# Attention masked by bias products in two batches instead of one, with another order of loads, copies and first products

## The chip, the cores and the metric

The kernel runs on one core of one Trainium2 chip. The metric is device time in microseconds (us). Three runs of the kernel before took 254.89, 254.92 and 255.02 us; the median is 254.92 us.

## The reference

The inputs are q, k and v of 8 batches, 8 heads, 576 positions and 64 values per head, and four matrices. All are float32. Cut to what matters:

```python
scores = matmul(q, k.T) / sqrt(64)
rel = pos[:, None] - pos[None, :]
mask_plain = (rel >= 0) & (rel < 32)                       # heads 0 to 3
mask_dil = (rel >= 0) & (rel < 128) & (rel % 4 == 0)       # heads 4 to 7
attn = softmax(where(mask, scores, -1e9))
x = matmul(attn, v)          # as 4608 tokens x 512
a, b = x @ w1, x @ w2        # 512 -> 1024
out = ((a * b) @ w3) @ w_out # 1024 -> 1024 -> 512
```

Each position sees 32 keys only: the last 32 (plain heads) or every fourth of the last 128 (dilated heads).

## The kernel before

**The layout.** The positions of each head are sorted by their remainder modulo 4, so that a dilated window becomes a run of 32 neighbours. Both kinds of heads are then cut into blocks of 96 queries that see 128 keys (96 and a halo of 32). A batch has 12 such blocks: six for the four plain heads (u = 0), six for the four dilated heads (u = 1). All multiplications are done in bfloat16.

**The work on a batch.** q, k and v are loaded by DMAs that the POOL queue issues and that convert to bfloat16. Batch 0's first halves of q and k come as float32 over the SP queue and are rounded by ScalarE. VectorE turns them (`turn`, L388 and L403: transposes of 32x32 blocks) so that the head's values lie across partitions. In batches 0 and 1, v is turned by VectorE too, then turned back by TensorE against an identity (`v_back`, L412), and copied to `vps` (`v_keep`: L422 on ScalarE, L424 on VectorE); these are the tasks VK. From batch 2 on (`DIRECT_V = 2`), v is loaded straight into place by many small DMAs.

TensorE makes scores for a group of blocks in four PSUM banks (`Group.scores`, L454). ScalarE takes the exponential (L465). A step is three blocks, four heads: TensorE multiplies the exponentials with v and a column of ones (`values`, L490), VectorE takes the reciprocal of the sums (L501) and scales (L513). In batches 0 and 1 (`TURNED = 2`) TensorE turns the step back (L530) and a copy puts it into the matrix of tokens XT (`Step.keep`: L538 on ScalarE, L540 on VectorE); these are the tasks K. From batch 2 on, a DMA issued by SP does it (L543).

**The masks.** There are two ways. Batches under `BIASED` are grouped by three blocks, and a matmul of the identity with a table of 0 and -30000 (`bias`) is put into the PSUM banks ahead of the scores (L437), so that the exponential of a masked score is 0. The other batches are grouped by five blocks across batch borders (`GRP = 5`), and VectorE multiplies the exponentials with a 0/1 mask, in two halves (L473). POOL makes that mask from the bias table (L367). The choice is made here:

```python
if biased:
    first = {(0, 0): 0, (0, 3): 1, (1, 0): 4, (1, 3): 4}[self.blocks[0][1:]]
    for g in range(4):
        nc.tensor.matmul(out=self.sp[:, g, 0 : self.n * QB], lhsT=ident,
            rhs=bias[:, first : first + self.n, :], start=True, stop=False)
...
if b < BIASED:
    for i in range(0, 12, 3):
        group(every[i : i + 3], True)
```

**The products.** w3 and w_out are multiplied once on the chip (w3 is turned by L647, copied by L654, multiplied by L659, and kept as `wf_sb` by L670 on ScalarE or L672 on VectorE; the tasks W3D). The tokens are worked off in 16 units of 288 columns, two for a batch. For each unit and each of eight pieces of 128 outputs, TensorE makes the up products a and b (L563, four matmuls of 288 columns each, over the four pieces of XT: two of plain heads, two of dilated heads), ScalarE copies a (L573), VectorE multiplies with b (L578). Down products of 128 tokens (L589, eight matmuls of 512 columns) follow when their gates and all of `wf_sb` are there; ScalarE copies them (L600) and SP stores them.

**What sets the order.** All instructions are recorded as tasks with a duration, dependences and a rank. A planner (`Plan.run`) takes, whenever an engine is free, the ready task of the lowest rank, gives out the eight PSUM banks, and puts filler matmuls (L701) where TensorE would be idle ahead of the first up product. The tasks are then written out in this order, and each engine takes its queue strictly in it. The constants at the head of the file steer it: `RANK` and `FIRST` give ranks by kind of task (`FIRST` for batch 0; E exponential, VK and K the copies, N reciprocal and scaling, T turns, VT v turned back, S scores, V values, X step turned back), `WARM` counts matmuls at the start (L684), `FIRST_LOADS` and `B0_LOADS` set the order of loads on POOL ("v10" is batch 1's v, first half; "w0" a piece of w1 and one of w2; "o0" half of w_out; "30" the first 128 rows of w3), `ON_DVE` names copies that VectorE makes, `HALVED` copies of which ScalarE makes one half and VectorE the other. `LEAD` sets which up products must go ahead of a batch's scores. `PARTED` is 0: an up product waits for all four pieces of XT.

```python
if k or parted == PARTED:
    return add(name, "PE", 490, need + wl, lambda: up(k, f, key), seq, slot=1,
               after=after), []
...
for b, i, t in paced:
    pair = int(16 * (b - LEAD) + 4 * i)
```

Of the kernel before, what the change touches and what calls it, by code (L numbers as in the profile page):

```python
# [19 lines left out]
S = 576  # L20
# [6 lines left out]
UNIT = 288  # L27
RING = 1152
BIG = 30000.0
BIASED = 1  # L30
LATE = False
TURNED = 2
DIRECT_V = 2
ORDER = (2, 3, 0, 1)
RES = (0, 2, 1, 3)
RANK = dict(E=0.5, VK=3, K=2, N=0.2, T=0.5, VT=0.05, S=0.1, V=0.05, X=0.1, W=0.5, C=5)
FIRST = {"E": 3, "VK": 1, "K": 0.2, "N": 2, "T": 0.2, "VT": 0.05, "S": 0.3, "V": 0.1, "X": 0.3}
WARM = 25
FILL = 110
FIRST_LOADS = ("30", "w0", "v10", "w1", "w2", "31", "k10", "q10", "o0", "o1", "32", "33", "34", "q11", "k11", "v11", "35", "36", "37")  # L40
SHIFT = {}
ON_DVE = ("K0.2", "VK0.1.1", "W3D1", "W3D4", "W3D5")
GRP = 5
WHOLE = ("qn", "kn")
B0_LOADS = ("v0", "q1", "k1", "v1")
HALVED = ("K0.0", "K0.1", "K0.3", "K1.1", "VK0.0.0", "VK0.1.0", "VK1.0.1", "VK1.1.0")
MASK_AT = 19.5
PARTED = 0
BUSY = 4500
LEAD = 1.1  # L50


class Task:
# [10 lines left out]
class Plan:  # L64
# [10 lines left out]
    def add(self, name, eng, dur, deps, fn, prio, slot=0, lat=150, after=()):  # L75
        t = Task(name, eng, dur, deps, fn, prio + SHIFT.get(name, 0), slot, lat, after)
        self.tasks.append(t)
        return t
# [108 lines left out]
def kernel(  # L187
# [51 lines left out]
    def bank(n, dtype=F32):  # L239
        at = ps[:, plan.now.place or 0, :]  # L240
        return (at if dtype == F32 else at.bitcast(dtype))[:, 0:n]
# [317 lines left out]
    def up(k, f, key, chunks=ORDER, first=True, last=True):  # L559
        if first:  # L560
            held[(key, k, f)] = bank(UNIT)
        for j, c in enumerate(chunks):
            nc.tensor.matmul(  # L563
                out=held[(key, k, f)],
                lhsT={"a": w1_sb, "b": w2_sb}[key][:, c, f * P : (f + 1) * P],
                rhs=unit_cols(k, c),
                start=(first and j == 0),
                stop=(last and j == len(chunks) - 1),
            )
# [74 lines left out]
    def w3_back(ft):  # L644
        x = bank(KFF * P, BF16).rearrange("p (g x) -> p g x", g=KFF)
        for g in range(KFF):
            nc.tensor.transpose(  # L647
                out=x[:, g, :], in_=w3n[ft][:, g * P : (g + 1) * P], identity=ident
            )
        held[("x3", ft)] = x  # L650

    def w3_keep(ft):
        w3T[ft] = wk_pool.tile([P, KFF, P], BF16, tag="w3T", bufs=3, name="w3T")
        nc.scalar.copy(out=w3T[ft], in_=held[("x3", ft)])  # L654
# [13 lines left out]
    def w3_done(ft, eng):  # L668
        if eng == "ACT":
            nc.scalar.copy(out=wf_sb[:, ft, :], in_=held[("wf", ft)])  # L670
        else:
            nc.vector.tensor_copy(out=wf_sb[:, ft, :], in_=held[("wf", ft)])  # L672
# [5 lines left out]
    def rank(kind, b):  # L678
        return (RANK if b else FIRST)[kind]

    def warm_up():
        o = bank(256)
        for i in range(WARM):
            nc.tensor.matmul(out=o, lhsT=warm[:, 0:P], rhs=warm, start=True, stop=True)  # L684
# [21 lines left out]
    c0 = add("const2", "DVE", 1400, [c1], constants, -98)  # L706
    add("warm", "PE", 700 + 213 * WARM, [c1], warm_up, 0)

# [11 lines left out]
    def loads_rows(nm, b, us=None):  # L720
        old = turned.get((nm, b - 2), [])
        for u in (0, 1) if us is None else us:
            L[(nm, b, u)] = None
        sl = slice(0, 2) if us is None else slice(us[0], us[-1] + 1)
        t = load(f"L{nm}{b}", 700, 3100 if us is None else 1600, old,
                 lambda: load_rows(nm, rows_of[nm], b, sl))
        for u in (0, 1) if us is None else us:
            L[(nm, b, u)] = t
# [25 lines left out]
    plan.dma = 1200 + 1350 * len(WHOLE)  # L754
    for x in B0_LOADS:
        loads_rows(x[0] + "n", 0, (int(x[1]),))
# [9 lines left out]
    lw12 = {}  # L766
    for x in FIRST_LOADS:
        c = int(x[1])
# [12 lines left out]
    for ft in sorted(lw3):  # L781
        x = add(f"W3T{ft}", "PE", 450, [lw3[ft], idt], lambda f=ft: w3_back(f), RANK["W"], slot=1,
                after=w3m[-3:-2])
        y = add("W3C", "ACT", 1012, [x], lambda f=ft: w3_keep(f), RANK["C"], lat=100, after=w3m[-3:-2])
        if ft + 7 in lw3:
# [4 lines left out]
        name = f"W3D{ft}"  # L790
        eng, dur = ("DVE", 688) if name in ON_DVE else ("ACT", 585)
        FUSED.append(add(name, eng, dur, [z], lambda f=ft, e=eng: w3_done(f, e), -1, lat=100))
# [28 lines left out]
    for b in range(B):  # L821
# [9 lines left out]
        for u in range(2):  # L831
# [3 lines left out]
            for half in range(2):  # L835
# [5 lines left out]
                name = f"VK{b}.{u}.{half}"  # L841
                eng, dur = ("DVE", 980) if name in ON_DVE else ("ACT", 880)
                ways = [(eng, dur, slice(0, 4))]
                if name in HALVED:
                    ways = [("ACT", 540, slice(0, 2)), ("DVE", 560, slice(2, 4))]
# [44 lines left out]
        every = [(b, u, m) for u in range(2) for m in range(6)]  # L890
        if b < BIASED:
            for i in range(0, 12, 3):
# [8 lines left out]
        while steps < 4 * B:  # L901
# [25 lines left out]
            if bb < TURNED:  # L927
                x = add("X" + n, "PE", 310, ns + [idt], st.back, bb - 99 + rank("X", bb), slot=1)
                name = f"K{n}"
                eng, dur = ("DVE", 460) if name in ON_DVE else ("ACT", 640)  # L930
                ways = [(eng, dur, slice(0, 6 * QB))]
                if name in HALVED:
                    ways = [("ACT", 400, slice(0, 3 * QB)), ("DVE", 270, slice(3 * QB, 6 * QB))]
# [14 lines left out]
    def ups(k, f):  # L948
# [8 lines left out]
        def product(key, after):  # L957
# [3 lines left out]
            seq += 1  # L961
            if k or parted == PARTED:
                return add(name, "PE", 490, need + wl, lambda: up(k, f, key), seq, slot=1,
# [47 lines left out]
    for b, i, t in paced:  # L1011
        pair = int(16 * (b - LEAD) + 4 * i)
        if pair > 0:
# [38 lines left out]
```

## Time and profile before

| what | value |
| --- | --- |
| median of three runs | 254.92 us |
| profiled execution: time | 255.02 us |
| profiled execution: span | 253.2 us |
| granted TensorE clock, mean | 0.998 |
| busy: PE / DVE / ACT / POOL | 245.8 / 167.9 / 124.3 / 67.8 us |
| matmuls | 2760 |
| up products L563 | 1024 matmuls, first at 20.27 us, last at 244.0 us |
| bias products L437 | 16 matmuls |
| mask passes L473 | 34, 21.2 us |
| exponentials L465 | 21, 34.2 us |
| DMA | 33.40 MB, 210 GB/s until about 50 us |

Spans and starts are counted from the first instruction of the profile. "Busy" is the time in which at least one instruction of an engine runs; matmuls overlap, so that the mean of one is longer than its share of the time. A row of the groups names the line, engine and operation, what it writes and reads, how often it stands, its busy time, the mean duration of one in ns, and the idle time of its engine just before it with what ended most of that.

### The profile page before, as it was taken

The page shows a single profiled execution, that of the slowest core. Times are in us where ns is not written, and L with a number is a line of the kernel's source. Part 1 is how long each engine was busy: PE and PEld are TensorE (multiplying, and loading weights), DVE is VectorE, ACT ScalarE, POOL GpSimd, SP SyncE. Part 2 cuts the span into 40 slices and gives each one's busy share as a digit, 9 for nine tenths or more (in the row PEclk, how much of TensorE's full clock was granted, in tenths as well). Part 3 has the DMA queues.
Part 4 walks back from the last instruction along what each step waited for, and adds up shares of the span by engine and source line. Part 5 has one row for each costly group of instructions (what it writes and reads, how often), then busy time and mean ns, then how long its engine had stood idle before and what let it go on. Part 6 is the DMA issues. An engine that isn't in the chain of part 4 may idle for free.

```text
span 253.2 us, 6818 instructions
## 1 busy us (share of the span) xinstructions
PE 245.8 (97%) x2760; PEld 170.6 (67%) x2760; DVE 167.9 (66%) x350; ACT 124.3 (49%) x221; POOL 67.8 (27%) x106
## 2 busy tenths in 40 slices
PE   7889999999999999999999999999999999999994
PEld 5668876565767676677676766676767666777662
DVE  3998657697898887588868977837737365333321
ACT  5664555766635534362626526356353643333331
POOL 7635835343614432303250310800000000000000
PEclk9999999999999999999999999999999999999999
DMA  7999999999997999998799667862332223311114
GB/s 226 204 200 209 207 210 211 208 107 184 220 168 121 189 170 208 235 95 114 122 202 110 89 77 104 137 84 65 67 65 67 67 67 67 104 36 51 41 41 124
DMA packets 59422, 33.40 MB, mean 132 GB/s; under 512 B 44800, under 2 KB 49280, under 8 KB 59392
## 3 DMA queue, kind: packets, MB, share of 16 engines
q0 software_dynamic: 38592, 18.81, 58.7%
q1 hardware_dynamic: 20656, 14.10, 24.3%
q8 instruction: 21, 0.34, 0.6%
q14 instruction: 9, 0.07, 0.1%
q10 hardware_dynamic: 144, 0.07, 0.1%
HBM read 38.80 MB, written 9.44 MB: 190 GB/s over the span
## 4 chain that ended last, share of the span: by engine, by line
PE 90%; DVE 5%; DMA 2%; issue 1%; ACT 1%; ACTq 0%; DVEq 0%
PE ps L563 49%; PE ps L589 24%; PE ps L659 6%; PE ps L490 4%; PE ps L454 4%; DMA gt<-in_q_dram 2%; DVE qt L403 1%; DVE xo L513 1%; PE ps L647 1%; PE ps L607 1%; PE ps L701 1%; PE ps L530 1%; ACT qn L278 0%; DVE et L473 0%; PE ps L412 0%
## 5 line engine op out<-in xcount | busy, mean ns | idle before, releaser
L563 PE MATMUL ps<-XT,w_sb 128*128 128x288 bf16 x1024 | 136.3, 286 | 0.0
L563 PEld LDWEIGHTS <-w_sb 128*128 128x128 bf16 x1024 | 97.8, 98 | 30.6
L578 DVE TENSOR_TENSOR gt<-ps,asb 128x288 bf16<-128x288 f32 x128 | 57.5, 454 | 49.0 <-PE ps L563 46.7
L573 ACT CAST asb<-ps 128x288 bf16<-128x288 f32 x128 | 50.7, 398 | 49.3 <-PE ps L563 46.0
L589 PE MATMUL ps<-wf_sb,gt 128*128 128x512 bf16 x280 | 65.8, 379 | 0.0
L600 ACT COPY osb<-ps 128x512 f32<-128x512 f32 x35 | 20.5, 585 | 55.1 <-PE ps L589 55.0
L589 PEld LDWEIGHTS <-gt 128*128 128x128 bf16 x280 | 27.2, 98 | 26.9
L300 POOL DMA_DIRECT2D vp<-in_v_dram x48 | 30.3, 639 | 48.3 <-PE ps L490 30.3
L465 ACT ACTIVATE et<-ps 128x1920 bf16<-128x1920 f32 (+2 forms) x21 | 34.2, 1633 | 7.7 <-PE ps L454 5.5
L513 DVE TENSOR_TENSOR xo<-ps,rcp 96x384 bf16<-96x384 f32 (+1 forms) x48 | 31.4, 675 | 0.5
L473 DVE TENSOR_TENSOR et<-et,mask 128x960 bf16<-128x960 bf16 (+1 forms) x34 | 21.2, 645 | 6.8 <-ACT et L465 6.7
L403 DVE STREAM_TRANSPOSE qt<-qn 128x320 uint32<-128x320 uint32 (+3 forms) x34 | 22.3, 670 | 2.1 <-ACT qn L278 1.8
L490 PEld LDWEIGHTS <-et 128*128 128x128 bf16 x384 | 14.6, 98 | 1.9 <-issue 0.4
L490 PE MATMUL ps<-vp,et 128*128 128x65 bf16 x384 | 15.5, 193 | 0.1
L659 PE MATMUL ps<-wo_sb,w3T 128*128 128x512 bf16 x64 | 15.0, 379 | 0.1
L403 DVE STREAM_TRANSPOSE kt<-kn 128x320 uint32<-128x320 uint32 (+3 forms) x18 | 11.6, 646 | 4.5 <-PE ps L454 4.3
L454 PEld LDWEIGHTS <-kt 32*128 32x128 bf16 x768 | 9.1, 92 | 5.9 <-issue 4.7
L454 PE MATMUL ps<-qt,kt 32*128 32x96 bf16 x768 | 12.1, 201 | 0.7 <-DVE kt L388 0.7
L501 DVE RECIPROCAL rcp<-ps 96x12 f32<-96x12 f32 x32 | 6.9, 218 | 8.3 <-PE ps L490 8.0
L286 POOL DMA_DIRECT2D vp<-in_v_dram x6 | 7.2, 1194 | 11.5 <-PE ps L490 10.7
L659 PEld LDWEIGHTS <-w3T 128*128 128x128 bf16 x64 | 5.9, 98 | 6.3 <-issue 0.3
L388 DVE STREAM_TRANSPOSE kt<-kn 128x576 uint32<-128x576 uint32 (+1 forms) x9 | 9.9, 1121 | 0.2 <-PE ps L454 0.2
(56 smaller groups left out, 117.6 us busy)
## 6 DMA issues: line engine op xcount, KB each, us to landing
qn<-in_q_dram POOLq DMA_DIRECT2D x6, 576.0 KB, 8.2
kn<-in_k_dram POOLq DMA_DIRECT2D x6, 576.0 KB, 9.0
w3n<-in_moe_w_dram POOLq DMA_DIRECT2D x8, 256.0 KB, 11.2
out_dram<-osb SPq DMA_DIRECT2D x7, 256.0 KB, 3.0
out_dram<-osb SPq DMA_DIRECT2D x8, 224.0 KB, 2.9
vp<-in_v_dram POOLq DMA_DIRECT2D x6, 288.0 KB, 9.2
out_dram<-osb SPq DMA_DIRECT2D x8, 192.0 KB, 2.9
out_dram<-osb SPq DMA_DIRECT2D x8, 160.0 KB, 3.2
```

The costliest lines, as they stand in the source:

```text
L300: nc.gpsimd.dma_start(out=vp[32 + p0 : 32 + p0 + n, 4:8, m, 0:D], in_=v_rows(b, 4, 4 * t0 + res, [[4 * D, n], [S * D, 4], [1, D]]),)
L403: nc.vector.transpose(out=o, in_=i)
L454: nc.tensor.matmul(out=self.sp[:, g, QB * i : QB * i + QB], lhsT=kt[prt, u, QB * m : QB * m + P, c], rhs=qq, start=(c == 0 and not biased) ...
L465: nc.scalar.activation(out=ev, in_=self.sp[:, :, 0:x], func=ACT.Exp, scale=scale)
L473: nc.vector.tensor_tensor(out=ev, in0=ev, in1=mk, op=AL.mult)
L490: nc.tensor.matmul(out=self.o[:, g, mm, :], lhsT=grp.et[:, c0 : c0 + P], rhs=vps[self.b % 2][:, 4 * self.u + g, 3 * self.hf + mm, 0 : D + ...
L513: nc.vector.tensor_tensor(out=dst, in0=self.o[0:QB, hs, :, 0:D], in1=self.rcp[0:QB, hs, :].unsqueeze(3).to_broadcast([QB, n, 3, D]), op=AL ...
L563: nc.tensor.matmul(out=held[(key, k, f)], lhsT={"a": w1_sb, "b": w2_sb}[key][:, c, f * P : (f + 1) * P], rhs=unit_cols(k, c), start=(first ...
L573: nc.scalar.copy(out=a_sb, in_=held[("a", k, f)])
L578: nc.vector.tensor_tensor(out=gt[:, f, c0 : c0 + UNIT].rearrange("p (r m t) -> p m r t", r=2, m=BLK), in0=held[("b", k, f)].rearrange("p ( ...
L589: nc.tensor.matmul(out=y, lhsT=gt[:, f, c0 : c0 + P], rhs=wf_sb[:, f, :], start=(f == 0), stop=(f == KFF - 1),)
L659: nc.tensor.matmul(out=o, lhsT=w3T[ft][:, g, :], rhs=wo_sb[:, g, :], start=(g == 0), stop=(g == KFF - 1),)
```

## The change

Only constants at the head of the file change. Their effects:

- `BIASED` 2: batch 1 is masked by bias products, in four groups of three blocks; the groups of five then begin with batch 2.
- `FIRST_LOADS`: the first pieces of w1 and w2 go ahead of the first w3 rows; the three inputs of batch 1, each in two halves as before, go behind w_out and most of w3. `B0_LOADS`: the second half of batch 0's k goes ahead of the others.
- `PARTED` 3: the first three up products are made in two parts, the plain heads' pieces of XT first.
- `HALVED` and `ON_DVE`: other copies are shared between ScalarE and VectorE. Batch 0's copies K are whole on ScalarE, but for K0.2, which stays whole on VectorE. Batch 1's K1.0 and K1.1 and the VK copies VK0.0.0, VK1.0.1, VK1.1.0 and VK1.1.1 are made in halves, K1.3 whole on VectorE. VectorE keeps four pieces of `wf_sb` in place of three. (A name that stands in both lists is halved.)
- `RANK`, `FIRST`: other ranks; `WARM` 28 matmuls at the start for 25; `LEAD` 1.3 for 1.1.

```diff
-BIASED = 1
+BIASED = 2
...
-RANK = dict(E=0.5, VK=3, K=2, N=0.2, T=0.5, VT=0.05, S=0.1, V=0.05, X=0.1, W=0.5, C=5)
-FIRST = {"E": 3, "VK": 1, "K": 0.2, "N": 2, "T": 0.2, "VT": 0.05, "S": 0.3, "V": 0.1, "X": 0.3}
-WARM = 25
+RANK = dict(E=0.2, VK=0.2, K=1, N=1, T=0.3, VT=0.05, S=0.4, V=0.2, X=0.4, W=0.5, C=5)
+FIRST = {"E": 0.5, "VK": 0.2, "K": 3, "N": 0.3, "T": 1.5, "VT": 0.05, "S": 0.3, "V": 0.2, "X": 0.05}
+WARM = 28
...
-FIRST_LOADS = ("30", "w0", "v10", "w1", "w2", "31", "k10", "q10", "o0", "o1", "32", "33", "34", "q11", "k11", "v11", "35", "36", "37")
+FIRST_LOADS = ("w0", "30", "w1", "w2", "o0", "31", "o1", "32", "33", "v10", "34", "q10", "k10", "q11", "35", "v11", "36", "k11", "37")
...
-ON_DVE = ("K0.2", "VK0.1.1", "W3D1", "W3D4", "W3D5")
+ON_DVE = ("K0.2", "K1.0", "K1.1", "K1.3", "VK1.0.1", "VK1.1.0", "W3D0", "W3D3", "W3D4", "W3D6")
...
-B0_LOADS = ("v0", "q1", "k1", "v1")
-HALVED = ("K0.0", "K0.1", "K0.3", "K1.1", "VK0.0.0", "VK0.1.0", "VK1.0.1", "VK1.1.0")
+B0_LOADS = ("k1", "v0", "q1", "v1")
+HALVED = ("K1.0", "K1.1", "VK0.0.0", "VK1.0.1", "VK1.1.0", "VK1.1.1")
...
-PARTED = 0
+PARTED = 3
...
-LEAD = 1.1
+LEAD = 1.3
```

## The prediction

> **What bounds the kernel now.** I read the page's busy times and slices first, then the chain of waits, then busy time by stretches, then groups by shape, then instructions in order of time around the places that the change touches.
>
> The page's busy times, slices and two costliest groups:
> ```profile
> PE 245.8 (97%) x2760; PEld 170.6 (67%) x2760; DVE 167.9 (66%) x350; ACT 124.3 (49%) x221; POOL 67.8 (27%) x106
> ...
> PE   7889999999999999999999999999999999999994
> ...
> L563 PE MATMUL ps<-XT,w_sb 128*128 128x288 bf16 x1024 | 136.3, 286 | 0.0
> ...
> L589 PE MATMUL ps<-wf_sb,gt 128*128 128x512 bf16 x280 | 65.8, 379 | 0.0
> ```
> TensorE is the bound; only the first slices (6.3 us each) are not full. The 286 ns is from issue to end; matmuls overlap, so what one costs is the distance of starts. In the chain of waits 48 up products take 5.88 us: 0.1226 us each. In the same way a 512-column product costs 0.216, a values product 0.0305, a 128-column transpose 0.056, a 96-column one 0.043.
>
> The chain of waits (start, length, what), around the first up products:
> ```profile
> 13.26 0.51 PE ps L412 x6
> ...
> 15.50 0.23 DVE rcp L501
> 15.73 2.60 DVE xo L513 x4
> 18.33 0.23 DVE XT L540
> 18.59 0.41 ACT XT L538
> ...
> 19.74 0.37 PE ps L490 x12
> 20.11 0.33 PE ps L701 x3
> 20.44 1.47 PE ps L563 x12
> ```
> The three first steps of batch 0 are scaled one after the other from 15.73 on, and only then can products start; L701 is filler.
>
> Busy time by stretches (PE, PEld, DVE, ACT, POOL, each with its count):
> ```profile
> 8.70:14.00 5.30, 4.75 (x121) 3.80 (x121) 5.13 (x13) 4.36 (x5) 2.76 (x4) 1.00 1.21 203
> 14.00:18.00 4.00, 3.16 (x71) 2.31 (x69) 3.78 (x10) 1.97 (x3) 1.37 (x3) 1.00 1.34 200
> 18.00:22.00 4.00, 3.87 (x56) 3.28 (x54) 3.73 (x10) 1.71 (x5) 1.74 (x3) 1.00 1.29 205
> 22.00:34.00 12.00, 12.00 (x113) 9.82 (x111) 8.31 (x16) 6.72 (x15) 7.95 (x11) 1.00 1.20 209
> ```
> VectorE is full until 14 us. Filler counts as busy here, so I work the idle time out. From 8.7 to 22 us the timeline has 4 score groups (0.47 each, below), 12 bias products, 24 V transposes, 48 values products, 8 w3 transposes, 24 back transposes and 12 up products: 1.88+1.47+1.34+1.46+0.45+1.03+1.47 = 9.10 of 13.3 us. So 4.2 us are wait or filler. The same count over 22 to 62 us leaves 0.54, of which 0.28 lie at 38 us and 0.23 at 52. After that there is next to none. Call the sum N: 4.2+0.54 = 4.75 us. The time is TensorE's work plus N plus what both kernels share (8.7 us of start, 4 us of end).
>
> **The change part by part.**
>
> *Bias products for batch 1* (BIASED 2). Groups by shape and a piece of the timeline:
> ```profile
> L473 DVE TENSOR_TENSOR et<-et,mask 128x960 bf16<-128x960 bf16 x32 | 20.1, 651 | 6.4 <-ACT et L465 6.3
> ...
> L465 ACT ACTIVATE et<-ps 128x1152 bf16<-128x1152 f32 x4 | 4.4, 1129 | 3.5 <-PE ps L454 1.8 <-DVE xo L513 1.6
> ...
> L437 PE MATMUL ps<-bias,ident 128*128 128x288 bf16 x16 | 2.9, 286 | 0.7 <-DVE xo L513 0.5 <-ACT w3T L654 0.3
> ```
> ```profile
> 11.51 0.65 PE L437 MATMUL ps<-bias,ident 128*128 128x288 bf16 x4
> 12.10 0.44 PE L454 MATMUL ps<-qt,kt 32*128 32x96 bf16 x24
> 12.47 0.54 PE L490 MATMUL ps<-vp,et 128*128 128x65 bf16 x12
> ...
> 29.49 6.04 PE L563 MATMUL ps<-XT,w_sb 128*128 128x288 bf16 x48
> 35.47 0.62 PE L454 MATMUL ps<-qt,kt 32*128 32x96 bf16 x40
> 36.02 2.13 PE L563 MATMUL ps<-XT,w_sb 128*128 128x288 bf16 x16
> ```
> Batch 1 leaves the groups of five blocks and gets four groups of three, each with four products of 288 columns: 16 x 0.1226 = +1.96 us of TensorE work. They wait for four free banks, and behind them in TensorE's queue stand their own scores, then values. Scores are regrouped: the last bias product starts at 11.51+3x0.1226 = 11.88, a next one could start at 12.00, the values start at 12.47, so a group of 24 costs 0.47; by the lower three rows (35.37 to 36.02) one of 40 costs 0.65, hence 0.011 a matmul above a fixed part. Before: 4 of 24, 16 of 40, one of 32 (0.56) = 12.84. After: 8 of 24, 14 of 40, one of 16 (0.38) = 13.24; +0.40. Off the path: VectorE loses four mask passes (0.651 each), ScalarE goes from 21 exponentials (34.2 us) to 23 (about 34.6). As VectorE ends no wait of TensorE past 62 us, I price these at nothing; without that cover they would give back at most 2.6 us of VectorE time in batch 1 to 7. On the path: **+2.36 us**.
>
> The Trainium skill, "TensorE: Matmul & The Clock Gate", section "Back-to-back issue gap", says that in a stream of weight loads and matmuls the spacing sinks to about 131 ns at 512 columns and 81 at 128; between these, an estimate from that page, 288 columns would cost 102 ns, the 16 products 1.6 us and the forecast would be 0.3 lower. The rows here say 216, 56 and 122.6 ns, so the row stands.
>
> *Order on VectorE at the start* (RANK, FIRST, B0_LOADS, HALVED, ON_DVE). All instructions of batch 0 stay, their places change. Ahead of the first scaling stand today, from 8.5 us, a whole V turn, twelve part turns (0.41 to 0.47) and two V copies (0.55). In the new order it stands behind eight part turns and one copy: 4 x 0.44 + 0.55 = 2.3 us earlier, at 13.4. I then walked the written order with the rows' durations, each engine taking its queue in order. Second scaling 15.7 (0.94 long); third scores 13.5, exponential 14.0 to 15.1, a V copy on ScalarE that is now whole (0.81 for 0.48) to 15.8, values 16.7, scaling 17.6 to 18.6, turned back by 19.0, copied by VectorE (0.45) by 19.5: first whole up product at 19.55, back to back from there, and (PARTED 3) four half products from 18.3 on. Copies K0.0, K0.1 and K0.3 are whole again on ScalarE (0.64 for 0.40, +0.24 each); that is inside the walk. By 22.0 there are 24 up products: 4 + 2.45/0.1226. Work from 8.7 to 22 is then 9.10 + 12 x 0.1226 less 6 back transposes that come just later (0.26) = 10.3, N here 3.0 instead of 4.2: -1.2. The same walk over the old order gives 4.6 where the trace has 4.2, so it runs slow; set against itself it says -1.6. I take **-1.4** (N here 2.8). Bounds: nothing gained, or all 2.9 us that lie between 14 and 22.
>
> *The parted products* wait for one operand less in front, and the second parts wait at 19.5 for the VectorE copy. Behind them in TensorE's queue stand only other up products that need the same copy. No further cost.
>
> *Warm-up* 28 for 25. The timeline has these at 0.213 us until 6.66 us and 0.109 from there: the three more end by about 7.0, and the first scores wait for K until 8.7. Nothing. The wait in front of these scores grows from 0.94 to about 1.35 us, because less filler stands there. The same page, section "What's actually happening", has the clock halved after an idle window of about 3.4 us; no such wait stands in the new order, and no stretch here shows a granted clock under 1.00 at the start, so the sum is the same by either.
>
> *Loads* (FIRST_LOADS, B0_LOADS). POOL issues the same DMAs, batch 1 in three pairs of halves in both kernels; only places move, and SP's loads stay. Today's half loads land 1.37 us apart and w3 rows 1.25. w1 and w2 move in front of the first w3 row and land about 1.3 earlier (14.8); needed at 18.3. Batch 1 goes behind w_out and w3: its first V half lands near 34 (turned at 37.5), its first K half near 38 (43.7), its last near 45 (51.7). Batch 0's second K half comes first on POOL (lands 7.6, turned 8.5); the others land 0.4 to 0.5 before their turns, as one does today. POOL's mask work (4.75 us at 24) stays between loads with eight still under way. So nothing, with 3 us of cover for batch 1.
>
> *Batch 1's chain comes later.* Today its pieces lie between up products from 35 us on. In the new order all of batch 0's products but two are done by 35, then w3 work runs, and batch 1's four groups start at 45.6 and 55 with little to put between: exponential 46.7 to 47.8, values at 48.0 after 0.5 us of wait; exponential 56.0 to 57.1, values at 57.3 after 0.4; first down product 0.2 behind a wf copy at 60.3; small ones 0.1. N from 22 to 62: 1.2 for 0.54: **+0.6**. Bounds: zero wait (-0.54), and one more exponential for each of the four groups (4 x 1.13 = +4.5); I stay near the walk, since on the old order it gives 0.53 here where the trace has 0.54. Batch 1's V and K copies in halves or on VectorE, and four wf copies there (0.69) for three, lie in it.
>
> *LEAD* 1.3 lets later scores run 3 up pairs sooner; past 62 us nothing waits today, so nothing.
>
> Sum: +2.36 - 1.4 + 0.6 = +1.6, and 0.2 off for short waits after 62 us that the new order does not repeat: **+1.4 us**. The profiled execution took 255.02 (span 253.2 and 1.8 around it), so 256.4; the median of the runs is 0.10 below it: **256.3**.
>
> **The rivals.** In terms of N (2.8 + 1.2 forecast) the change of time is 2.36 - (4.75 - N), less the 0.2.
>
> 1. *Up products cover TensorE's waits from 14 us on* (other side). The start then keeps only the 1.3 us that today lie between 8.7 and 14, and the lead feeds TensorE through batch 1 as today (0.54): N = 1.84, 2.36 - 2.91 - 0.2 = -0.75: 254.2. It decides from N below 2.1. For it speaks that VectorE, full until 14, is relieved there; against it the chain exponential, V copy, values, scaling, copy, whose rows alone take the first whole product to 19.5.
> 2. *Start better by half, batch 1 dearer by half only*: N = 2.1 + 0.8 = 2.9, +0.3: 255.2, no change to be measured. For it: the walk ran 0.4 slow on the old order.
> 3. *Batch 1 late*: from 49 to 63 us the new order has no up product, so each delay of that chain is paid whole. One turn pair (0.75+0.65) late on VectorE, whose queue there is nearly full, puts 1.4 on top: 257.7. Against it: the loads' 3 us of cover.
> 4. *The change does little*: the halves of batch 1 exist already, six matmuls of 1024 are parted. Then the extra work alone is left, +2.36: 257.3.
>
> **How the numbers follow.** Forecast 0.66, rival 1 0.06, 2 0.12, 3 0.10, 4 0.06. 0.2% is 0.5 us, about what a measurement of this kernel can tell from no change. Faster 0.06, within it 0.12, slower 0.82. The range runs from rival 2 to rival 4: 255.1 to 257.4, with rival 1 and most of 3 outside.
>
> **What would show it.** Right: 2776 matmuls, 32 of them L437, the scores 0.4 us dearer; first up product near 18.3 and 24 by 22 us; no up product between about 49 and 63, waits of about 0.5 at 47 and 57 behind exponentials; solid TensorE from 63 on. Wrong: N under 3.1 (start before 18, no waits at 47 and 57), or a long wait of TensorE on a turn or a landing between 45 and 62, or waits after 70.

## The result and the profile after

The changed kernel takes 256.45 us (median of four runs, 256.42 to 256.48). The kernel before took 254.97 us beside it (four runs, 254.89 to 255.04). The ratio is 1.0058, with a 95% interval from 1.0041 to 1.0076: slower by 1.48 us.

The page's span, busy times, slices and two groups, after:
```profile
span 254.7 us, 6842 instructions
...
PE 247.6 (97%) x2776; PEld 171.7 (67%) x2776; DVE 164.9 (65%) x345; ACT 124.5 (49%) x222; POOL 68.2 (27%) x106
...
PE   7799999999999999999999999999999999999994
...
L465 ACT ACTIVATE et<-ps 128x1920 bf16<-128x1920 f32 (+2 forms) x23 | 34.3, 1506 | 9.3 <-PE ps L454 8.6
...
L473 DVE TENSOR_TENSOR et<-et,mask 128x960 bf16<-128x960 bf16 (+1 forms) x30 | 18.5, 631 | 4.2 <-ACT et L465 4.0
```
The bound is the same: TensorE at 97%, and only the first two slices of the span and the last are not full. There are 16 matmuls more than before. VectorE lost 3.0 us of busy time and ScalarE gained 0.2; the sum below closes without a term for either. Of the groups by shape, this is the one that the prediction prices (16 matmuls before):
```profile
L437 PE MATMUL ps<-bias,ident 128*128 128x288 bf16 x32 | 5.3, 287 | 0.0
```
Busy time by stretches (PE, PEld, DVE, ACT, POOL, each with its count; then granted clock, DMA share, GB/s), after:
```profile
8.70:14.00 5.30, 4.73 (x115) 3.44 (x116) 4.99 (x12) 3.38 (x5) 2.77 (x4) 1.00 1.28 203
14.00:18.00 4.00, 4.00 (x92) 3.54 (x90) 3.48 (x9) 3.98 (x5) 1.67 (x3) 1.00 1.35 198
18.00:22.00 4.00, 4.00 (x51) 3.37 (x49) 3.00 (x8) 2.87 (x6) 1.19 (x3) 1.00 1.25 208
40.00:50.00 10.00, 9.74 (x144) 6.37 (x142) 7.38 (x13) 6.34 (x8) 4.39 (x7) 1.00 1.11 212
56.00:62.00 6.00, 5.68 (x80) 3.14 (x77) 5.82 (x13) 3.51 (x5) 5.21 (x8) 1.00 1.01 151
```
From 14 to 18 us TensorE is now full where it had 3.16 us of 4; part of that is filler. What is new is idle time late: 0.26 us between 40 and 50 us and 0.32 between 56 and 62. The chain of waits shows the place of both (start, length, what):
```profile
18.43 0.24 PE ps L563 x2
18.68 0.26 PE ps L530 x6
18.94 0.25 PE ps L563 x2
...
46.20 0.40 PE ps L454 x23
...
46.62 1.14 ACT et L465
...
47.81 0.54 PE ps L490 x12
...
55.84 1.14 ACT et L465
...
57.02 0.54 PE ps L490 x12
...
59.59 0.59 ACT wf_sb L670
...
60.22 1.89 PE ps L589 x8
```
The first lines hold the first two half products, two matmuls each, with a step turned back between. (A piece of the chain begins where the piece before it ends, so these lines stand 0.16 us behind the starts.) The whole products come next. In the order of time on TensorE, by starts:
```profile
18.27 0.41 PE L563 MATMUL ps<-XT,w_sb 128*128 128x288 bf16 x2
...
19.50 2.61 PE L563 MATMUL ps<-XT,w_sb 128*128 128x288 bf16 x20
```
The later lines of the chain are batch 1's two pairs of groups: scores, an exponential of 1.14 us, values, with TensorE waiting for the end of the exponential, and the first down product behind a `wf_sb` copy.

Counted as the prediction counts it (work by distances of starts, N the time of TensorE that is wait or filler), with the same prices for both kernels (the prediction's own count had 4.2 and 0.54 before):

| us | before | after | difference | forecast |
| --- | --- | --- | --- | --- |
| more matmuls: 16 x 0.1226 and regrouped scores | | | +2.36 | +2.36 |
| N, 8.7 to 22 us | 4.26 | 3.07 | -1.19 | -1.4 |
| N, 22 to 62 us | 0.54 | 0.92 | +0.38 | +0.6 |
| N after 62 us | 0.21 | 0.16 | -0.05 | -0.2 |
| sum | | | +1.50 | +1.4 |

The spans differ by 1.5 us and the medians by 1.48. After 62 us no single wait is over 0.1 us in either kernel, so that row is a sum of very small ones. The first row is counts by prices; that these microseconds are really paid is tested below.

### The profile page after: what moved, and what is told of

The parts are those of the page before. It is cut to its first block, busy times and chain, and to the rows that moved or that the text cites. A ratio compares the mean times of both kernels' runs of the same rounds, so it can differ in the third digit from the quotient of the medians.

```text
span 254.7 us, 6842 instructions
## 1 busy us (share of the span) xinstructions
PE 247.6 (97%) x2776; PEld 171.7 (67%) x2776; DVE 164.9 (65%) x345; ACT 124.5 (49%) x222; POOL 68.2 (27%) x106
## 4 chain that ended last, share of the span: by engine, by line
PE 93%; DVE 2%; ACT 2%; DMA 2%; issue 0%; ACTq 0%; DVEq 0%
PE ps L563 50%; PE ps L589 24%; PE ps L659 5%; PE ps L490 5%; PE ps L454 4%; DMA gt<-in_q_dram 2%; PE ps L647 1%; PE ps L412 1%; ACT et L465 1%; PE ps L437 1%; PE ps L530 1%; PE ps L607 1%; DVE qt L403 1%; PE ps L701 1%; ACT qn L278 0%; DVE vt L388 0%
## 5 line engine op out<-in xcount | busy, mean ns | idle before, releaser
L578 DVE TENSOR_TENSOR gt<-ps,asb 128x288 bf16<-128x288 f32 x128 | 58.1, 455 | 62.6 <-PE ps L563 61.1
L473 DVE TENSOR_TENSOR et<-et,mask 128x960 bf16<-128x960 bf16 (+1 forms) x30 | 18.5, 631 | 4.2 <-ACT et L465 4.0
L252 POOL DMA_DIRECT2D qn<-in_q_dram x9 | 5.9, 654 | 13.8 <-DVE qt L403 10.6
```

The lines of the kernel that those rows point to most:

```text
L578: nc.vector.tensor_tensor(out=gt[:, f, c0 : c0 + UNIT].rearrange("p (r m t) -> p m r t", r=2, m=BLK), in0=held[("b", k, f)].rearrange("p ( ...
```

## The experiments

All experiments replace the 24 DMAs that turn the steps of batches 2 to 7 by two plain DMAs each of the same bytes, on the same queue at the same place. So the tokens of these batches are not turned, and the output of these batches is not the reference's. Two runs measure what this replacement does by itself, and the others are compared with these two.

```diff
-            nc.sync.dma_start_transpose(
-                out=self.cols().rearrange("p (i x) -> p i x", i=6),
-                in_=self.xo[0:QB, :],
-            )
+            n = 6 * QB
+            nc.sync.dma_start(out=self.cols()[0:QB, :], in_=self.xo[0:QB, 0:n])
+            rest = self.xo[0 : P - QB, 12 * D - n :]
+            nc.sync.dma_start(out=self.cols()[QB:P, :], in_=rest)
```

**The replacement on both kernels** (plain_before, plain_after)

> The kernel before with one replacement that all further kernels share: the turned steps of batches 2 to 7 (24 DMA transposes, L543) are moved to XT by two plain DMAs each, 96 and 32 partitions, and so not transposed; their output rows mean nothing. TensorE, VectorE, ScalarE and POOL keep their instructions and their order. As TensorE waits for none of these DMAs past 62 us: within 0.3 us of 254.97.

> The changed kernel with the same replacement (batches 2 to 7 moved untransposed). Within 0.3 us of 256.45, and 1.3 to 1.6 us above plain_before.

Measured: 254.94 us (254.88 to 255.28, ten runs) and 256.55 us (256.45 to 257.75, five runs, of which four lie from 256.45 to 256.59). The kernel before had 255.01 on this chip, and on the two other chips used below. The ratios are 0.9999 (0.9990 to 1.0009) and 1.0059 (1.0042 to 1.0076). The replacement changes nothing that can be measured, and the difference is kept: 1.61 us. The one run of 257.75 is taken up at the end.

### Are the bias products on the path?

The prediction priced all 16 matmuls as paid, beside the waits at 47 and 57 us. A rival reading is that these waits would be there without them, or longer, so that part of the 1.96 us fills time that TensorE waits anyway. Two runs keep the changed order and change only the number of bias products in batch 1. The first leaves them out (batch 1 is then not masked at all), the second makes them twice (its mask is then -60000).

```diff
-            self.sp = ps[:, plan.now.place : plan.now.place + 4, :]
+            self.sp = ps[:, plan.now.place : plan.now.place + 4, :]; biased = biased and self.blocks[0][0] != 1
```


> plain_after in its own order (batches 2 to 7 untransposed as there), but the 16 bias products of batch 1 are left out, so batch 1 is not masked: all 128 keys of a block count. If each of them is on the path (the prediction): -16 x 0.1226 = -1.96 us against plain_after. If only the first four of each pair of groups are, because the second four stand where TensorE would wait for the exponential of the first: -8 x 0.1226 = -0.98 us, with the waits at 47 and 57 us longer. If all of them fall into waits: no change.

```diff
-                for g in range(4):
+                for j, g in [(j, g) for j in range(1 + self.blocks[0][0]) for g in range(4)]:
...
-                        start=True,
+                        start=(j == 0),
```


> plain_after in its own order (batches 2 to 7 untransposed as there), each of the 16 bias products of batch 1 made twice into the same bank (twice the table: masked scores stay masked, others get 0 twice). If each is on the path: +1.96 us against plain_after. If the second four of each pair first use up the waits of 0.36 and 0.56 us that follow: +1.0 to +1.1 us, and those waits gone.

Measured: without them 255.44 us (255.35 to 255.64, ten runs), 1.1 less than plain_after; twice 257.71 us (257.67 to 257.83), 1.16 more. In each direction 1.96 us of matmuls moved the time by a little over half.

TensorE's instructions in order of time, without the bias products (start, length; in brackets the idle time before and what ended it):
```profile
45.69 0.48 PE L454 MATMUL ps<-qt,kt 32*128 32x96 bf16 x27
46.73 0.42 PE L454 MATMUL ps<-qt,kt 32*128 32x96 bf16 x21 [0.56 <-DVE wf_sb L672]
47.37 0.54 PE L490 MATMUL ps<-vp,et 128*128 128x65 bf16 x12 [0.22 <-ACT et L465]
...
55.27 0.44 PE L454 MATMUL ps<-qt,kt 32*128 32x96 bf16 x24 [0.41 <-DVE wf_sb L672]
56.09 0.54 PE L490 MATMUL ps<-vp,et 128*128 128x65 bf16 x12 [0.39 <-ACT et L465]
```
The same with them twice:
```profile
46.96 1.15 PE L437 MATMUL ps<-bias,ident 128*128 128x288 bf16 x8
48.04 0.44 PE L454 MATMUL ps<-qt,kt 32*128 32x96 bf16 x24
48.42 0.54 PE L490 MATMUL ps<-vp,et 128*128 128x65 bf16 x12
```
Without the products, the second group of each pair comes to its banks too early and waits 0.56 and 0.41 us for a VectorE copy of `wf_sb`, and the values still wait for the exponential. With twice as many, the wait ahead of the values at 48 us is gone: the second group's products cover the first group's exponential. So in the changed kernel the products of the second group of each pair stand where TensorE would wait. This doesn't change the sum of the prediction, since its waits were worked out with the products in place; it changes what each part is worth by itself.

### Masks or products, with the order of each kernel

> plain_before (batches 2 to 7 moved untransposed) with batch 1 masked by bias products and nothing else changed; the planner lays the order out anew. Theory (TensorE's work and its waits add up): 2.36 us of work on top; the written order, followed with the durations of the old rows, has 0.53 us more of waits from 22 to 62 us and the start unchanged: +2.8 us against plain_before. Rival (the bias products fall where TensorE waits anyway, the loss comes from batch 1 being loaded late): under +1.0 us.

> plain_after (batches 2 to 7 untransposed) with batch 1 masked by VectorE as in the kernel before, all else as changed; the order is laid out anew. Prediction's reading (the bias products are 2.36 us of work, VectorE's mask passes cost nothing): -2.4 us against plain_after. Rival (with batch 1 behind the up products of batch 0, the exponential of five blocks and the mask passes lie on the path, so the bias products pay for themselves): the written order followed with the old rows' durations has waits of 3.2 us between 45 and 62 us and 3.4 after 62, where plain_after has 1.2 and 0.1: +2.8 us.

The edits are one line each, `BIASED = 2` in the order of before and `BIASED = 1` in the changed one. The planner orders the tasks anew for each.

Measured: bias products in the old order 257.94 us (257.80 to 258.15), 3.0 more than plain_before. With the 2.36 us of work paid in full, 0.6 are left over. The trace shows some of that as idle time of TensorE, 0.27 us in each of two stretches, where the kernel before has 0.10 and 0.08 (5.90 and 5.92 us busy):
```profile
34.00:40.00 6.00, 5.73 (x105) 4.18 (x103) 3.26 (x9) 3.35 (x5) 2.43 (x4) 1.00 1.13 211
50.00:56.00 6.00, 5.73 (x101) 4.37 (x94) 3.14 (x7) 5.72 (x8) 2.25 (x4) 1.00 1.58 121
```
That is 0.36 us; where the rest of the 0.6 lies isn't shown. Masks in the new order 259.11 us (259.03 to 259.21), 2.56 **more** than plain_after. The reading that the masks would give the 2.36 us of work back falls.

Stretches of masks in the new order (masks_back_2, columns as above):
```profile
40.00:50.00 10.00, 8.27 (x99) 4.78 (x98) 7.39 (x12) 5.93 (x7) 4.37 (x6) 1.00 1.11 211
50.00:56.00 6.00, 5.53 (x97) 3.81 (x95) 4.65 (x9) 4.76 (x6) 1.75 (x3) 1.00 1.58 120
62.00:70.00 8.00, 6.73 (x129) 4.35 (x127) 5.72 (x10) 5.75 (x7) 5.15 (x7) 1.00 1.00 188
80.00:100.00 20.00, 18.78 (x228) 12.05 (x227) 17.87 (x33) 8.94 (x14) 7.85 (x12) 1.00 1.11 170
```
and two places of its TensorE in order of time:
```profile
46.77 0.61 PE L647 MATMUL ps<-ident,w3n 128*128 128x128 bf16 x8
49.11 1.90 PE L659 MATMUL ps<-wo_sb,w3T 128*128 128x512 bf16 x8 [1.74 <-ACT w3T L654]
...
67.33 0.62 PE L454 MATMUL ps<-qt,kt 32*128 32x96 bf16 x40 [1.27 <-ACT et L465]
```
TensorE is idle for 1.7, 0.5, 1.3 and 1.2 us in these four stretches. At 49 us it waits for a w3 copy on ScalarE, whose queue holds the exponential of a group of five blocks ahead of it; at 67 us a group of scores waits for the exponential that holds its banks. In this order no up product stands between 47 and 65 us, so a group of five with its exponential of 1.77 us and its mask passes finds little on TensorE beside it. That the mask passes themselves, rather than the longer exponentials, end these waits isn't seen: both rows name ScalarE.

### Does an earlier first up product count in full?

The prediction takes a start that is earlier by 1.2 to 1.4 us as that much off the time. A rival would be that a later stage has slack and only passes on part. This run puts 11 filler matmuls of 256 columns (0.109 us each, 1.2 in all) ahead of the first up product of the changed kernel.

```diff
-            held[(key, k, f)] = bank(UNIT)
+            held[(key, k, f)] = bank(UNIT); [nc.tensor.matmul(out=held[(key, k, f)][:, 0:256], lhsT=warm[:, 0:P], rhs=warm, start=True, stop=True) for _ in range(11 if (key, k, f) == ('a', 0, 0) else 0)]
```


> plain_after in its own order (batches 2 to 7 untransposed), with 11 filler matmuls of 256 columns (0.109 us each) put in TensorE's queue ahead of the first up product: the lead of 1.2 us that the new start gives is taken away. If the lead counts at its face: +1.2 us against plain_after. If the waits of batch 1 at 47 and 57 us would have eaten it: +0.2 to +0.4 us, and those waits smaller by as much.

Measured: 257.72 us (257.65 to 258.00), 1.17 more than plain_after. The lead counts at its face value. The stretch around the late waits, with the 11 matmuls:
```profile
40.00:50.00 10.00, 9.74 (x131) 6.03 (x129) 6.67 (x11) 6.31 (x8) 4.36 (x6) 1.00 1.11 211
56.00:62.00 6.00, 5.68 (x104) 3.57 (x103) 5.66 (x11) 3.57 (x5) 5.03 (x7) 1.00 0.94 139
```
These are the 9.74 and 5.68 us of the changed kernel: the late waits did not shrink, which fits waits between exponentials and values that all moved together.

### The new start with masks, and work held back for batch 1

If the start is worth 1.2 us and the products cost 2.36, the start with masks and with up products kept for the time of batch 1 should beat both kernels. This run has masks for batch 1, `PARTED = 3`, `WARM = 28`, the weights first among the loads, and ranks and added times of due (`SHIFT`, 30 entries) that, among others, hold some of unit 1's up products back (A1.3, A1.5, A1.7, A1.4, B1.0). It is compared with plain_before.

```diff
-RANK = dict(E=0.5, VK=3, K=2, N=0.2, T=0.5, VT=0.05, S=0.1, V=0.05, X=0.1, W=0.5, C=5)
-FIRST = {"E": 3, "VK": 1, "K": 0.2, "N": 2, "T": 0.2, "VT": 0.05, "S": 0.3, "V": 0.1, "X": 0.3}
-WARM = 25
+RANK = {'E': 7, 'VK': 2, 'K': 1.5, 'N': 0.3, 'T': 0.02, 'VT': 0.5, 'S': 1, 'V': 3, 'X': 1.5, 'W': 0.05, 'C': 0.05}
+FIRST = {'E': 5, 'VK': 3, 'K': 7, 'N': 1.5, 'T': 3, 'VT': 0.02, 'S': 0.02, 'V': 2, 'X': 0.2}
+WARM = 28
...
-FIRST_LOADS = ("30", "w0", "v10", "w1", "w2", "31", "k10", "q10", "o0", "o1", "32", "33", "34", "q11", "k11", "v11", "35", "36", "37")
-SHIFT = {}
-ON_DVE = ("K0.2", "VK0.1.1", "W3D1", "W3D4", "W3D5")
+FIRST_LOADS = ('w0', '30', '31', 'w1', '32', 'v10', 'o0', 'o1', 'w2', 'q10', 'k10', 'q11', '33', '34', '35', '36', 'v11', 'k11', '37')
+SHIFT = {'S1.1.0': 22.3, 'VK1.1.0': 17.0, ... 'A1.3': 29.3, ... 'A1.5': 21.6, ... 'A1.7': 21.8, 'B1.0': 15.2, 'A1.4': 16.2, ...}
+ON_DVE = ('K0.2', 'K0.3', 'K1.0', 'K1.1', 'K1.2', 'K1.3', 'VK0.0.0', 'VK1.0.0', 'VK1.1.0', 'W3D1', 'W3D2', 'W3D6')
...
-B0_LOADS = ("v0", "q1", "k1", "v1")
-HALVED = ("K0.0", "K0.1", "K0.3", "K1.1", "VK0.0.0", "VK0.1.0", "VK1.0.1", "VK1.1.0")
+B0_LOADS = ('v0', 'k1', 'q1', 'v1')
+HALVED = ('K0.0', 'K1.2', 'VK0.0.0', 'VK0.1.1')
...
-PARTED = 0
+PARTED = 3
...
-LEAD = 1.1
+LEAD = 1.06
```


> A version sought for both: one batch of bias products as before (16 matmuls), the changed start (first three products in two parts, w1 and w2 first), and ranks that keep up products of batch 0 back, so that they stand between the groups of batch 1 (batches 2 to 7 untransposed as in plain_before). Theory: TensorE's work as before, waits from 8.7 to 22 us of 2.7 us where the old order has 4.6, and 0.0 from 22 to 62 where it has 0.5: -2.4 us against plain_before, about 252.6. Rival (the lead can't be had without the bias products): not under plain_before.

Measured: 253.20 us (253.01 to 253.37), ratio 0.9930 (0.9915 to 0.9945); 1.74 less than plain_before and 3.35 less than plain_after, where 2.4 less than plain_before was expected. Its stretches:
```profile
14.00:18.00 4.00, 3.95 (x87) 3.45 (x85) 3.79 (x9) 2.76 (x5) 1.79 (x3) 1.00 1.27 201
40.00:50.00 10.00, 10.00 (x147) 7.44 (x146) 8.19 (x16) 8.28 (x11) 4.96 (x7) 1.00 1.12 212
56.00:62.00 6.00, 6.00 (x72) 3.06 (x74) 5.40 (x10) 1.77 (x4) 2.30 (x4) 1.00 0.88 120
```
TensorE is full through batch 1, on masks, and the first up product starts at 18.16 us (20.27 in the kernel before, 18.27 in the changed one). So the early start doesn't need the bias products, and masks aren't worse in every order; in masks_back_2 they stood in another order of the work. Of the expected gain 0.7 us is missing. Some 0.3 of that lies in the expectation: it took 4.6 us of waits at the start for the old order, as the walk gives, where the trace has 4.26. The rest stays open. The constants were changed together, so none of them is tested alone; which of them brings the early start, here and in the changed kernel, isn't shown either.

### The warm-up

The prediction costs 28 warm-up matmuls for 25 at nothing, because TensorE waits for K until 8.7 us in any case. Two runs change the number to 14 and to 45.

```diff
-        for i in range(WARM):
+        for i in range(WARM - 14):
```


> plain_after in its own order (batches 2 to 7 untransposed), with 14 warm-up matmuls for 28, so that TensorE idles for about 3 us ahead of the first scores. One run of plain_after took 257.75 us where the others took 256.45 to 256.59; in its profile the clock had risen early, TensorE idled for 2.2 us ahead of the first scores, and the granted clock was 0.50 from 12 to 14 us. If that idle time halves the clock: about 1.3 us or more above 256.52 in most runs, a granted clock near 0.5 somewhere between 9 and 15 us. If the clock fell for another reason: within 0.3 us of 256.52.

```diff
-        for i in range(WARM):
+        for i in range(WARM + 17):
```


> plain_after in its own order (batches 2 to 7 untransposed), with 45 warm-up matmuls for 28: about 1.9 us more of them, to about 8.9 us. If idle time ahead of the first scores halves the clock: no run 1 us above the others, and the time 0.1 to 0.5 us above 256.52, since the first scores start at 8.9 in place of 8.7. If not: such runs stay possible.

Measured: 14 gives 257.10 us (257.02 to 257.18), 0.6 more than plain_after (0.5 or more in each of four runs), between the two readings of the expectation (1.3 or more, and within 0.3). 45 gives 256.47 (256.41 to 256.54), the same, where 0.1 to 0.5 more was expected: the first scores start at 8.74 us and not at 8.9. So more warm-up is free, less is not. The last section shows what goes with it in the traces.

## Why the prediction was right, step by step

The forecast was 256.3 us and the measurement 256.45, and the likeliest case is the one that came, by the mechanism that was forecast. That the number is so close is in part luck: three terms were off by about 0.2 us each, and the errors nearly cancel. Of its terms:

- **The added work, +2.36.** The counts are there: 2776 matmuls, 32 of L437. Right as a term of the sum. But "on the path" isn't right for each of the matmuls by itself: in the changed order nearly half of their time covers waits (no_bias_2 -1.1, bias_twice_2 +1.16 for 1.96). In the old order the time grew by more than their full price (bias_alone_2, +3.0).
- **The order at the start, -1.4.** The walk is confirmed in its details: four matmuls of half products from 18.27 (forecast 18.3), the first whole product at 19.50 (19.55), 24 matmuls of up products by 22 us, N 3.07 where the walk itself gave 3.0. What failed is the correction: the walk had been 0.4 off on the old order, and the forecast took another 0.2 off for that. The term measured -1.19. That it counts in full is shown by lead_back.
- **Batch 1's chain, +0.6.** The places are right: waits behind the exponentials at 47 and 57 us, the first down product at 60.2 behind a `wf_sb` copy, no up product from 49.3 to 62.9. The size is +0.38: values started at 47.81, forecast 48.0, and the "small ones" of 0.1 did not appear.
- **After 62 us, -0.2.** It was -0.05: short waits of 0.16 us in all remained, of 0.21. The forecast had taken all of it as gone, without a place.
- **VectorE's four mask passes, "at nothing".** The reason given (VectorE ends no wait of TensorE after 62 us) held for removing them: VectorE lost 3.0 us of busy time, and the sum closes without a term for it. The bound beside it, that they are worth at most 2.6 us of VectorE time, treats masks and products as a price that is the same in any order. It isn't: masks for products gain 3.0 us in the old order and lose 2.56 in the new one, each as the planner then lays it out, and in the new one TensorE waits for ScalarE behind the larger groups.
- **Warm-up and loads, nothing.** From 45 to 62 us TensorE waited for ScalarE alone, for no landing and no turn. The three more warm-ups delayed nothing (first scores at 8.65 us, 8.73 before), and 17 more were free too. The sentence that no wait stands there that could touch the clock was too sure. The wait forecast as 1.35 us (from the start of the last bias product to the first scores) was 1.09 in the changed kernel's profile and 2.44 in one run of plain_after, with consequences (last section). Nor does the clock of the stretches settle it: it reads 1.00 also where the prediction's own timeline has warm-up matmuls at 0.213 us, half the rate of those at 0.109.

The three errors: the start 0.2 us and the waits after 62 us 0.15 too favourable, batch 1's chain 0.2 too dear. Rival 1 (other up products cover the start's waits) asked for an N under 2.1 from 8.7 to 62 us, and N is 3.99 there; rival 2 asked for 2.9. Rival 4 needed no gain at the start; N fell by 1.19 there, and lead_back shows that this counts. Rival 3 needed a late turn or landing; none stands in the chain of waits.

## What to carry to other kernels

Count the bound engine's work by distances of starts, take the rest of the span as waits with a place and a releaser each, and forecast both separately; here the counted sum came to +1.50 us where the medians differ by 1.48. The way of masking had no price of its own here: the same switch was worth +3.0 us in one order of the work and -2.6 in the other, so it must be costed with the work that stands beside it. Where a long product stage can be spread, it is worth a try to keep some of it for the stretch in which a chain of short steps would leave the bound engine waiting. masks_spread did so, and TensorE had no wait there; how much of its gain comes from that alone isn't shown.

## What was not expected: the clock at the start

In the one run of plain_after that took 257.75 us, which is the profiled one, the warm-up matmuls reached full rate earlier than in the changed kernel's own profile. Its TensorE in order of time, and two stretches:
```profile
1.40 4.52 PE L684 MATMUL ps<-warm 128*128 128x256 bf16 x28 [1.40 <-DVE warm L688]
...
8.68 0.44 PE L454 MATMUL ps<-qt,kt 32*128 32x96 bf16 x24 [2.16 <-DVE kt L388]
```
```profile
10.00:12.00 2.00, 1.57 (x23) 1.31 (x15) 1.62 (x4) 1.32 (x2) 0.78 (x2) 0.73 1.26 193
12.00:14.00 2.00, 2.00 (x19) 1.57 (x18) 1.24 (x4) 1.18 (x2) 1.28 (x2) 0.50 1.40 205
```
In the changed kernel the same two rows read:
```profile
1.40 5.85 PE L684 MATMUL ps<-warm 128*128 128x256 bf16 x28 [1.40 <-DVE warm L688]
...
8.65 0.44 PE L454 MATMUL ps<-qt,kt 32*128 32x96 bf16 x24 [0.80 <-DVE kt L388]
```
The rise to full rate is read from the starts of the warm-up matmuls, which lie 0.213 us apart before it and 0.110 behind it: it came at 4.1 us in this run and at 6.8 in the changed kernel's profile. The early rise finished the warm-up 1.3 us sooner, the wait for K grew from 0.80 to 2.16 us, and then the granted clock fell to a half in the middle of the start, some 2 us after the scores had begun. The first up product came at 19.62 in place of 18.27, and the run was 1.2 us longer. Of the 27 executions that keep this start and its 28 warm-ups (after, plain_after, no_bias_2, bias_twice_2, lead_back), it is the only one so far above the others of its kernel. With 14 warm-ups the wait was 2.93 us, and the clock 0.89 from 8 to 10, 0.50 from 10 to 12 and 0.75 from 12 to 14 us:
```profile
8.68 0.44 PE L454 MATMUL ps<-qt,kt 32*128 32x96 bf16 x24 [2.93 <-DVE kt L388]
```
```profile
10.00:12.00 2.00, 1.91 (x30) 1.43 (x22) 1.54 (x4) 1.43 (x2) 0.78 (x2) 0.50 1.26 197
```
The first up product came at 19.03 us there. With 45 warm-ups no such wait is left and the clock stays at 1.00; four runs can't show that this keeps so rare a run away. Worked out from the clocks of the stretches (14 to 16 us has 0.92 in plain_after), the time at half clock is 1.08 + 2 + 0.32 = 3.4 us in one and 0.44 + 2 + 1.0 = 3.4 us in the other.

The Trainium skill, "TensorE: Matmul & The Clock Gate", section "What's actually happening", has a free-running window of 3413 ns and the half clock after at least one idle window. The 3.4 us at half clock agree with the length of that window, and a rise that comes earlier in one execution than in another agrees with a window that runs free. The condition differs: here idle times of 2.16 and 2.93 us, shorter than a window, were followed by the half clock. Idle times ahead of the same scores of 0.80 us (the changed kernel), 1.16 (no_bias_2), 1.52 (bias_twice_2) and 1.69 (plain_before) were not: the clock stays at 1.00 behind them. The row of the scores on plain_before's page:
```profile
L454 PE MATMUL ps<-qt,kt 32*128 32x96 bf16 x768 | 12.1, 201 | 1.7 <-DVE kt L388 1.7
```
So if the length of this idle time alone decided, the limit would lie between 1.69 and 2.16 us. Whether it does, or whether it also depends on where in the window the idle time falls, no run here shows.
